# Attention weights of blocks 4 to 17 transposed by VectorE in 32x32 squares and moved by DMAs, not by TensorE

## The chip, the cores and the metric

The kernel runs on one core of one Trainium2 chip. A core has several engines, each with its own instruction queue: TensorE (PE, with PEld for its weight loads) multiplies matrices, VectorE (DVE) and ScalarE (ACT) work on 128 lanes of data, as GpSimd (POOL) does, and SyncE (SP) issues DMAs. Engines wait for one another by semaphores. TensorE writes its products to PSUM; SBUF is the memory from which all engines work. The metric is the device time of one execution in microseconds (us); lower is better.

## What is computed

Attention over chunks of 64 tokens (8 batches, 8 heads, 576 tokens of 64 values per head), whose result is the input of a feed-forward layer with a rational function between its two products:

```python
scores = scale * np.matmul(q_c, k_c.transpose(0, 1, 2, 4, 3))
scores = scores - np.max(scores, axis=-1, keepdims=True)
attn = np.exp(scores)
attn = attn / (np.sum(attn, axis=-1, keepdims=True) + 1e-09)
out = np.matmul(attn, v_c)
...
h = x @ w_in
h2 = h * h
h3 = h2 * h
P = a[0] + a[1] * h + a[2] * h2 + a[3] * h3
Q = 1.0 + np.abs(b[0]) * np.abs(h) + np.abs(b[1]) * h2
g = P / (Q + 1e-06)
return (g @ w_out).astype(np.float32)
```

Here `x` has 4608 tokens of 512 values, `w_in` is 512 x 2048 and `w_out` 2048 x 512.

## The kernel before

**Tiling.** The 4608 tokens go in 18 blocks of 256. For the attention a block is 32 score matrices of 64x64, kept as one tile of 128 partitions x 1024 columns. Its feed-forward part goes in four steps, s = 0 to 3, of 512 hidden columns each. Products of the feed-forward layer use numbers split in a high and a low part, three products for one (`xhi`, `xlo` with `wi_hi`, `wi_lo`; `ghi`, `glo` with `wo_hi`, `wo_lo`).

**The order of work.** Every engine takes its instructions in the order in which the program writes them, and that order is written by hand as strings of letters. `START` orders the first twelve steps; from step (3,0) on, step (n,s) runs the letters of `STEADY[s]` (L668). Letters of the attention that belong to the next block, m = n+1, are `n N T K A X Y`; `S M U E0 E1` belong to block n+2; `w o s h l` finish block n-1; the others are the feed-forward work of the step itself or, for `Z z y`, of two steps before. So the attention of one block is spread over some two blocks of feed-forward work:

- `S`: 32 products of 64x64 make the scores `pss`; `M` and `U` reduce them to maxima, `E0` and `E1` write the exponentials to the tile `e`.
- `n` (L278, L279): the reciprocals of the row sums; `N` (L284): DVE multiplies `e` by them.
- `T` (L309): TensorE transposes `e` in eight 128x128 pieces into the PSUM tile `pst`; `K` (L313): ACT copies it to the SBUF tile `at`.
- `A` (L214): 32 products of 64x64 of `v` with `at` make `psx`; the load of the next block's `v` is issued behind it. `X` and `Y` split `psx` into `xhi` and `xlo`, with which the first step of block m starts.

**The end of a block.** For blocks 5 to 16 the last quarter of the second product is done with seven products instead of eight (letter `V`, `ff2_seven`), and its result `o` is put together by `w`, one ACT copy (L532) and four DVE adds of 256 columns (L533 to L536), and by `o`, a DVE add of 1024 columns (L541). For earlier blocks `store` copies a whole `o` by ACT (L577). In both cases `put` (L583) then stores `o` with four DMAs on SP's queue, each of 64 partitions.

**Shared buffers.** `e`, `at` and `o` are tiles of one tag, `eo`, that has two slots, taken in turn in the order in which the program makes the tiles. A new tile waits until whatever read or wrote the old one in its slot is done. The PSUM tiles `pst` and `xacc` share the tag `pa`.

Letters `Q I J p P g H R G Gp` are the rational function: L373 to L407 on DVE and ACT, with `Gp` (L407) on POOL.

Of the kernel before, what the change touches and what calls it, by code (L numbers as in the profile page):

```python
# [10 lines left out]
F32 = mybir.dt.float32  # L11
# [8 lines left out]
P = 128  # L20
# [4 lines left out]
NQ = UPB * NHP  # L25
# [32 lines left out]
def tile_chunked_attention_rational_moe(  # L58
# [11 lines left out]
    nc = tc.nc  # L70
    cp = ctx.enter_context(tc.tile_pool(name="cp", bufs=1))
    p2 = ctx.enter_context(tc.tile_pool(name="p2", bufs=2))
# [19 lines left out]
    def bank_pair(tag, name):  # L92
        return ps.tile([P, 2, 512], F32, tag=tag, name=name)


    loaded = {}

    def load_qk(n, early=False):
        if n >= NB:
            return  # L100
        if n > 5:
            if n == 6:
                loaded["qk"] = p2.tile([P, 2, W], F32, tag="raw", name="qk", bufs=3)
            loaded["q", n], loaded["k", n] = loaded["qk"][:, 0, :], loaded["qk"][:, 1, :]
        elif early:
            q, k = (p2.tile([P, W], F32, tag=t, name=f"{t}qk{n}") for t in "AB")
        else:
            qk = p2.tile([P, 2, W], F32, tag="raw", name=f"qk{n}", bufs=3)
            q, k = qk[:, 0, :], qk[:, 1, :]
        if n < 6:  # L110
            loaded["q", n], loaded["k", n] = q, k
        if not early:
            load_part(n, slice(0, W))
# [5 lines left out]
    def load_v(n):  # L119
        if n >= NB:  # L120
            return
        v = p2.tile([P, W], F32, tag="vt", name=f"v{n}", bufs=1)
        nc.sync.dma_start(out=v, in_=vP[n])
        loaded["v", n] = v
# [77 lines left out]
    def groups_of(u):  # L202
        return slice(0, NQ) if u is None else slice(u * NHP, (u + 1) * NHP)

    before, cuts = [""], [(0, 0)]

    def quarters(out_cols, tile_out, stat, mov, u):
        before[0] = "quarters"
        for g in range(NQ)[groups_of(u)]:
            for par in range(2):  # L210
                for c in range(2):
                    rows = slice(64 * c, 64 * c + 64)
                    cols = slice(g * 128 + par * 64, g * 128 + par * 64 + 64)
                    nc.tensor.matmul(  # L214
                        tile_out[par * 64:(par + 1) * 64, c, out_cols(g)],
                        stat[rows, cols], mov[rows, cols], start=True, stop=True,
                    )

    att = {}


    def have(key, n, make):
        if (key, n) not in att:
            att[key, n] = make()
        return att[key, n]

    def spread(x):
        return x.unsqueeze(3).to_broadcast([P, 2, x.shape[2], 64])

    def att_s(n, u=None, tag="pa"):  # L230
        pss = have("s", n, lambda: bank_pair(tag, f"pss{n}"))
        quarters(lambda g: slice(g * 64, g * 64 + 64), pss, loaded["q", n], loaded["k", n], u)
# [4 lines left out]
    def stats(n, u):  # L237
        st = have("st", n, lambda: p2.tile([P, 3, 2, NQ], F32, tag="sm", name=f"sm{n}"))
        return (st[:, i, :, groups_of(u)] for i in range(3))

    def exps(n, u):
        e = have("e", n, lambda: p2.tile([P, NQ, 2, 64], F32, tag="eo", name=f"e{n}"))
        return e[:, groups_of(u), :, :]

    def by_group(e):
        return e.rearrange("p h c k -> p c h k")
# [31 lines left out]
        nc.vector.tensor_scalar(rs, sm, 1e-9, WS, ALU.add, ALU.mult)  # L278
        nc.vector.reciprocal(rs, rs)  # L279

    def att_norm(n, u=None):
        ec = by_group(exps(n, u))
        _, _, rs = stats(n, u)
        nc.vector.tensor_mul(ec, ec, spread(rs))  # L284

    def att_norm_act(n):
        e, (_, _, rs) = exps(n, None), stats(n, None)
# [14 lines left out]
    def part(u):  # L302
        return slice(0, W) if u is None else slice(u * W // 2, (u + 1) * W // 2)

    def att_t(n, u=None, tag="pa"):
        e = att["e", n]
        pst = have("t", n, lambda: bank_pair(tag, f"pst{n}")).rearrange("p a b -> p (a b)")
        for g in range(NQ)[groups_of(u)]:
            nc.tensor.transpose(pst[:, g * 128:(g + 1) * 128], e[:, g, :, :].rearrange("p c k -> p (c k)"), ident)  # L309

    def att_copy(n, u=None):
        at = have("at", n, lambda: p2.tile([P, W], F32, tag="eo", name=f"at{n}"))
        nc.scalar.copy(at[:, part(u)], att["t", n].rearrange("p a b -> p (a b)")[:, part(u)])  # L313
# [3 lines left out]
    def att_av(n, u=None, tag="pa"):  # L317
        psx = have("x", n, lambda: bank_pair(tag, f"psx{n}"))

        def cols(g):  # L320
            v, hp = divmod(g, NHP)
            return slice(hp * 128 + v * 64, hp * 128 + v * 64 + 64)

        quarters(cols, psx, loaded["v", n], att["at", n], u)


    def x_views(n, u):
# [89 lines left out]
    def seven(n, s):  # L417
        return s == NST - 1 and ST_FIRST <= n < NB - 1
# [4 lines left out]
    def t_tile(name, dtype=F32R):  # L423
        return p2.tile([P, 4, 2, 256], dtype, tag="raw", name=name, bufs=3)
# [3 lines left out]
    def t_home(k):  # L428
        if k == 0:
            tw["hi"], tw["lo"] = t_tile("thi"), t_tile("tlo")  # L430
        tw["sum"] = p2.tile([P, 2, 2, 256], F32, tag="eo", name=f"tsum{k}")
# [67 lines left out]
    def s_lo(n, engine=None):  # L499
        slo[n] = p2.tile([P, 4, 2, 128], F32R, tag="xlo", name=f"slo{n}")  # L500
        (engine or nc.vector).tensor_sub(slo[n], sums.pop(n), shi[n].bitcast(F32))
# [73 lines left out]
    def store(n):  # L575
        o = p2.tile([P, 2, DM], F32, tag="eo", name=f"o{n}")
        nc.scalar.copy(o, obuf.pop(n))  # L577
        put(n, o)
# [26 lines left out]
    def ph_tag(g):  # L605
        return "p1" if g == 1 or (g >= 10 and g % 2 == 0) else "p0"
# [45 lines left out]
    def run(program, then=""):  # L652
# [13 lines left out]
    total = len(steps)  # L666
    one = lambda names, k: run(" ".join(f"{x}{k}" for x in names.split()))
    STEADY = (  # L668
# [4 lines left out]
    )  # L673

    def step(g):
        n, s = steps[g]
        m = n + 1 if n + 1 < NB else None
        early = n + 2 if n + 2 < NB else None
        whole, fast = seven(n, NST - 1), seven(n - 1, NST - 1)
        of_m = {  # L680
            "n": att_rs, "N": att_norm, "Na": att_norm_act, "T": att_t, "K": att_copy, "X": att_xhi, "Y": att_xlo,
            "A": lambda k: (att_av(k, tag=ph_tag(g + 1)), load_v(k + 1)),
        }
        of_early = {"S": lambda k: (att_s(k), load_qk(k + 1)), "M": att_max, "U": att_sub,
                    "E0": lambda k: att_exp_half(k, 0), "E1": lambda k: att_exp_half(k, 1)}
        of_prev = {"s": s_sums, "h": s_hi, "l": s_lo, "lp": lambda k: s_lo(k, nc.gpsimd), "w": s_store, "o": s_out}
        other = {"Q": chain_nq, "I": chain_nln, "g": chain_t, "H": chain_inv, "R": chain_g, "G": chain_split, "Gp": chain_split}
        tokens = STEADY[s].split()
        for token in tokens:
            name = token.rstrip("'")  # L690
            late = token != name
            k = g - 1 if late else g
            if name == "B":
                if n in (3, 4):
                    t_make(n - 3)
                continue
            if name == "K" and n in (3, 4):
                t_home(n - 3)
            if name in of_m:
                if m is not None:  # L700
                    of_m[name](m)
            elif name in of_early:
                if early is not None:
                    of_early[name](early)
            elif name in of_prev:
                if fast:
                    of_prev[name](n - 1)
            elif name == "V":
                if fast:
                    ff2_seven(n - 1)  # L710
                    run(f"y{g - LAG - 1}", "F")
                else:
                    run(" ".join(f"{x}{g - LAG}" for x in "Zzy"), "F")
                    store(n - 1)
            elif name in "Zzy":
                if not (s == 0 and fast and name == "y"):
                    last = "z" if s == 0 and fast else "y"
                    run(f"{name}{g - LAG}", "F" if name == last else "z")
            elif late and s == 0 and fast and name in other:
                other[name](*steps[k])  # L720
            elif late and s == 0 and fast and name in ("L", "Lp"):
                chain_rest(*steps[k], nc.gpsimd if name == "Lp" else None)
            elif name in ("L", "Lp"):
                pass
            elif not late and s == 3 and whole and name in other:
                other[name](*steps[k])
            elif late and g == FIRST:
                pass
            elif name == "Gp" and (g == FIRST or n == NB - 1):
                run(f"G{g}")  # L730
            else:
                run(f"{name}{k}")
# [45 lines left out]
```

## Time and profile before

| | us |
|---|---|
| median of three runs | 869.49 |
| lowest and highest | 869.23, 869.64 |
| span of the profiled execution, first to last instruction | 866.8 |
| median less span | 2.7 |
| DVE busy (753 instructions) | 764.2 |
| ACT busy (972) | 575.5 |
| POOL busy (50) | 109.8 |

The times are of three runs without the profiler; the profile and the trace are of one execution with it, for which the span is what was recorded. In the trace a row of a timeline has the start from the span's begin, the duration, the engine, the line of the kernel, the operation, output and inputs, the shape and how many instructions the row covers, and in brackets how long the engine had been idle and what ended that. The durations of matmuls overlap, since they are pipelined. SPq and ACTq are the queues of DMA issues.

### The profile page before, as it was taken

How to read it: one execution, taken by the hardware profiler on the slowest of the kernel's cores; microseconds unless marked ns; L12 is line 12 of the kernel's file. 1: busy time of each engine (PE TensorE's matmuls, PEld its weight loads, DVE VectorE, ACT ScalarE, POOL GpSimd, SP SyncE). 2: the span in 40 equal slices, each digit the busy share in tenths (PEclk: the TensorE clock that was granted, in tenths of full speed). 3: DMA queues.
4: the chain of work that ended last, by engine and by line, in shares of the span. 5: the costliest groups of instructions: out<-in, count | busy, mean ns of one | idle time of the engine just before them, and what ended most of it. 6: DMA issues, size and time to landing. Idle time of an engine off the chain costs nothing.

```text
span 866.8 us, 21128 instructions
## 1 busy us (share of the span) xinstructions
PE 850.7 (98%) x9312; PEld 839.8 (97%) x9312; DVE 764.2 (88%) x753; ACT 575.5 (66%) x972; POOL 109.8 (13%) x50
## 2 busy tenths in 40 slices
PE   4999999999999999999999999999999999999997
PEld 3899999999999999999999999999999999999997
DVE  6999998897888898989989898989898989899985
ACT  5999865755848665858485757576666758584643
POOL 1222222001212111010111111111111110101100
PEclk9999999999999999999999999999999999999999
DMA  8753304012121202011121212121202020101010
GB/s 315 268 217 125 122 26 147 26 26 74 25 75 25 75 1 85 15 50 51 25 75 25 74 26 74 26 74 26 74 22 78 1 76 24 43 9 25 2 26 26
DMA packets 16509, 55.90 MB, mean 64 GB/s; under 512 B 2592, under 2 KB 2592, under 8 KB 14368
## 3 DMA queue, kind: packets, MB, share of 16 engines
q1 hardware_dynamic: 16256, 54.28, 19.2%
q8 instruction: 73, 1.20, 0.6%
q10 hardware_dynamic: 160, 0.26, 0.1%
q14 instruction: 20, 0.16, 0.1%
HBM read 45.09 MB, written 9.44 MB: 63 GB/s over the span
## 4 chain that ended last, share of the span: by engine, by line
PE 93%; DVE 4%; DMA 2%; issue 0%; SPq 0%; ACT 0%; DVEq 0%
PE ph L357 44%; PE po L566 36%; PE xacc L523 4%; PE po L523 3%; PE psx L214 2%; PE pss L214 2%; PE pst L309 2%; DMA raw<-in_w_in 1%; DMA v<-in_vP 1%; PE pl L193 1%; DVE ghi L394 0%; DVE B L402 0%; DVE C L389 0%; DVE B L373 0%; DVE B L398 0%
## 5 line engine op out<-in xcount | busy, mean ns | idle before, releaser
L357 PE MATMUL ph<-xhi,wi_hi 128*128 128x256 f32 x1152 | 321.4, 279 | 0.0
L357 PE MATMUL ph<-xlo,wi_hi 128*128 128x256 f32 x1152 | 318.9, 277 | 0.3 <-DVE xlo L340 0.3
L357 PE MATMUL ph<-xhi,wi_lo 128*128 128x256 f32 x1152 | 318.6, 277 | 0.0
L357 PEld LDWEIGHTS ph<-xlo,wi_hi 128*128 128x128 f32 x1152 | 216.7, 188 | 0.7 <-DVE xlo L340 0.6
L357 PEld LDWEIGHTS ph<-xhi,wi_hi 128*128 128x128 f32 x1152 | 216.3, 188 | 0.9 <-issue 0.8
L357 PEld LDWEIGHTS ph<-xhi,wi_lo 128*128 128x128 f32 x1152 | 216.5, 188 | 0.0
L566 PE MATMUL po<-wo_hi,ghi 128*128 128x256 f32 (+2 forms) x920 | 181.3, 278 | 0.0
L566 PE MATMUL po<-wo_lo,ghi 128*128 128x256 f32 (+2 forms) x920 | 179.7, 277 | 0.0
L407 POOL TENSOR_TENSOR glo<-B,A 128x1024 fp32r<-128x1024 f32 x36 | 91.0, 2529 | 659.9 <-DVE B L402 633.6
L566 PEld LDWEIGHTS po<-wo_hi,ghi 128*128 128x128 f32 x920 | 138.7, 188 | 0.9
L566 PEld LDWEIGHTS po<-wo_lo,ghi 128*128 128x128 f32 x920 | 138.8, 188 | 0.0
L377 ACT ACTIVATE A<-B,cst 128x1024 f32<-128x1024 f32 x60 | 69.3, 1154 | 91.2 <-DVE B L373 86.1
L361 ACT ACTIVATE A<-ph,ab 128x1024 f32<-128x1024 f32 x72 | 81.7, 1134 | 62.6 <-PE ph L357 59.0
L566 PE MATMUL po<-wo_hi,glo 128*128 128x256 f32 (+2 forms) x920 | 114.9, 277 | 0.0
L566 PEld LDWEIGHTS po<-wo_hi,glo 128*128 128x128 f32 x920 | 109.1, 188 | 0.2
L394 DVE SCALAR_TENSOR_TENSOR ghi<-C,ab,A 128x1024 fp32r<-128x1024 f32 x60 | 77.0, 1283 | 25.1 <-ACT A L381 20.4
L369 ACT ACTIVATE C<-ph,ab 128x1024 f32<-128x1024 f32 x72 | 88.6, 1231 | 10.1 <-PE ph L357 10.1
L389 DVE SCALAR_TENSOR_TENSOR C<-C,ab,ph 128x1024 f32<-128x1024 f32 x72 | 92.2, 1281 | 3.1 <-ACT B L365 0.7
L373 DVE SCALAR_TENSOR_TENSOR B<-B,ab,A 128x1024 f32<-128x1024 f32 x60 | 79.6, 1328 | 10.4 <-POOL glo L407 5.3
L385 DVE TENSOR_TENSOR C<-C,ph 128x1024 f32<-128x1024 f32 x72 | 87.4, 1214 | 0.5 <-ACT A L361 0.4
L381 ACT ACTIVATE A<-A,cst 128x1024 f32<-128x1024 f32 x72 | 83.1, 1154 | 2.2
L402 DVE SCALAR_TENSOR_TENSOR B<-C,ab,B 128x1024 f32<-128x1024 f32 x60 | 77.0, 1284 | 1.9
(138 smaller groups left out, 1148.1 us busy)
## 6 DMA issues: line engine op xcount, KB each, us to landing
v<-in_vP SPq DMA_DIRECT2D x18, 512.0 KB, 4.0
out<-o SPq DMA_DIRECT2D x68, 128.0 KB, 2.4
raw<-in_w_in SPq DMA_DIRECT2D x8, 1024.0 KB, 6.3
raw<-in_w_out SPq DMA_DIRECT2D x8, 1024.0 KB, 4.8
qk<-in_qT SPq DMA_DIRECT2D x16, 512.0 KB, 5.1
qk<-in_kT SPq DMA_DIRECT2D x16, 512.0 KB, 6.0
Aqk<-in_qT SPq DMA_DIRECT2D x2, 256.0 KB, 5.2
Bqk<-in_kT SPq DMA_DIRECT2D x2, 256.0 KB, 5.5
```

The costliest lines, as they stand in the source:

```text
L357: nc.tensor.matmul(ph[:, fi, :], w[:, cc, f], x[:, cc, :], start=(k == 0), stop=(k == len(mm) - 1))
L361: nc.scalar.activation(ch[n, s][1], ch[n, s][0], AF.Abs, scale=b0)
L369: nc.scalar.activation(ch[n, s][3], ch[n, s][0], AF.Identity, bias=a2, scale=a3)
L373: nc.vector.scalar_tensor_tensor(B, B, b1a, A, ALU.mult, ALU.add)
L377: nc.scalar.activation(A, B, AF.Ln, bias=cst[:, 0:1], scale=2.0 ** -KLN)
L381: nc.scalar.activation(A, A, AF.Exp, bias=cst[:, 1:2], scale=-1.0)
L385: nc.vector.tensor_mul(C, C, h)
L389: nc.vector.scalar_tensor_tensor(C, C, a1, h, ALU.add, ALU.mult)
L394: nc.vector.scalar_tensor_tensor(gbuf[n, s][0], C, a0, A, ALU.add, ALU.mult)
L402: nc.vector.scalar_tensor_tensor(B, C, a0, B, ALU.add, ALU.subtract)
L407: (engine or nc.vector).tensor_mul(gbuf[n, s][1], B, A)
L566: nc.tensor.matmul(accs[n][i][:, cols], g[:, fi, i * 128:(i + 1) * 128], w[:, FPS * s + fi, cols], start=start, stop=stop,)
```

## The change

From the steady part on, that is for blocks 4 to 17, the transposing is taken from TensorE. `T` is now `att_turn`: one DVE instruction transposes `e` in squares of 32x32, each in place among its neighbours, and writes them to a new tile `et`. `K` is now `att_move`: sixteen DMAs on SP's queue, each of 32 partitions by 256 columns, bring the squares from `et` to their places in `at`. `A` reads `at` in two runs of 32 columns for one of 64 (`split`). The normalisation is done by POOL (`Np`), ahead of `T`. `T` and `K` stand in the second step (s = 1) rather than in the third: `T` ahead of `w` and `o`, `K` behind `o`. `D` is the part of the old `K` that makes a buffer for `t_make` in steps n = 3 and 4. `et` is a further tile of tag `eo`.

```diff
--- before.py
+++ after.py
@@ -204,7 +204,7 @@
 
     before, cuts = [""], [(0, 0)]
 
-    def quarters(out_cols, tile_out, stat, mov, u):
+    def quarters(out_cols, tile_out, stat, mov, u, split=False):
         before[0] = "quarters"
         for g in range(NQ)[groups_of(u)]:
             for par in range(2):
@@ -213,7 +213,8 @@
                     cols = slice(g * 128 + par * 64, g * 128 + par * 64 + 64)
                     nc.tensor.matmul(
                         tile_out[par * 64:(par + 1) * 64, c, out_cols(g)],
-                        stat[rows, cols], mov[rows, cols], start=True, stop=True,
+                        stat[rows, cols], mov[rows, 2 * par:2 * par + 2, g, :] if split else mov[rows, cols],
+                        start=True, stop=True,
                     )
 
     att = {}
@@ -278,10 +279,10 @@
         nc.vector.tensor_scalar(rs, sm, 1e-9, WS, ALU.add, ALU.mult)
         nc.vector.reciprocal(rs, rs)
 
-    def att_norm(n, u=None):
+    def att_norm(n, u=None, engine=None):
         ec = by_group(exps(n, u))
         _, _, rs = stats(n, u)
-        nc.vector.tensor_mul(ec, ec, spread(rs))
+        (engine or nc.vector).tensor_mul(ec, ec, spread(rs))
 
     def att_norm_act(n):
         e, (_, _, rs) = exps(n, None), stats(n, None)
@@ -308,6 +309,22 @@
         for g in range(NQ)[groups_of(u)]:
             nc.tensor.transpose(pst[:, g * 128:(g + 1) * 128], e[:, g, :, :].rearrange("p c k -> p (c k)"), ident)
 
+    def att_turn(n):
+        e = att["e", n].rearrange("p g c k -> p (g c k)")
+        t = p2.tile([P, 4, NQ, 32], F32, tag="eo", name=f"et{n}")
+        nc.vector.transpose(t.rearrange("p j g r -> p g j r"), e.rearrange("p (g j k) -> p g j k", j=4, k=32))
+        att["et", n] = t
+
+    def att_move(n):
+        t = att["et", n]
+        att["at", n] = at = p2.tile([P, 4, NQ, 32], F32, tag="eo", name=f"at{n}")
+        for j in range(4):
+            for i in range(4):
+                nc.sync.dma_start(out=at[32 * j:32 * j + 32, i, :, :], in_=t[32 * i:32 * i + 32, j, :, :])
+        turned.add(n)
+
+    turned = set()
+
     def att_copy(n, u=None):
         at = have("at", n, lambda: p2.tile([P, W], F32, tag="eo", name=f"at{n}"))
         nc.scalar.copy(at[:, part(u)], att["t", n].rearrange("p a b -> p (a b)")[:, part(u)])
@@ -321,7 +338,7 @@
             v, hp = divmod(g, NHP)
             return slice(hp * 128 + v * 64, hp * 128 + v * 64 + 64)
 
-        quarters(cols, psx, loaded["v", n], att["at", n], u)
+        quarters(cols, psx, loaded["v", n], att["at", n], u, n in turned)
 
 
     def x_views(n, u):
@@ -666,9 +683,9 @@
     total = len(steps)
     one = lambda names, k: run(" ".join(f"{x}{k}" for x in names.split()))
     STEADY = (
-        "F f Gp' s a L' h b l Q c n N I p J P g H R Gp Z z y",
-        "F f a b c V w o Q I p J P g H R G",
-        "F f a b c Q Z z y T K I p J P g H R Gp",
+        "F f Gp' s a L' h b l Q c n Np I p J P g H R Gp Z z y",
+        "F f a b c T V w o K Q I p J P g H R G",
+        "F f a b c Q Z z y D I p J P g H R Gp",
         "F f A S a b X Y c M B Q U I p J P E0 E1 g H R Z z y",
     )
 
@@ -678,7 +695,7 @@
         early = n + 2 if n + 2 < NB else None
         whole, fast = seven(n, NST - 1), seven(n - 1, NST - 1)
         of_m = {
-            "n": att_rs, "N": att_norm, "Na": att_norm_act, "T": att_t, "K": att_copy, "X": att_xhi, "Y": att_xlo,
+            "n": att_rs, "N": att_norm, "Np": lambda k: att_norm(k, engine=nc.gpsimd), "T": att_turn, "K": att_move, "X": att_xhi, "Y": att_xlo,
             "A": lambda k: (att_av(k, tag=ph_tag(g + 1)), load_v(k + 1)),
         }
         of_early = {"S": lambda k: (att_s(k), load_qk(k + 1)), "M": att_max, "U": att_sub,
@@ -694,8 +711,10 @@
                 if n in (3, 4):
                     t_make(n - 3)
                 continue
-            if name == "K" and n in (3, 4):
-                t_home(n - 3)
+            if name == "D":
+                if n in (3, 4):
+                    t_home(n - 3)
+                continue
             if name in of_m:
                 if m is not None:
                     of_m[name](m)
```

On DVE, block 9's steps 0 and 1 (the transposed block is 10; the names are those of the tiles, with a running number at the end). Before:

```order
L278 TENSOR_SCALAR sm_5371<-sm_5371 128x16
L279 RECIPROCAL sm_5371<-sm_5371 128x16
L284 TENSOR_TENSOR e_5379<-e_5379,sm_5371 128x2x8x64
L385 TENSOR_TENSOR C_0_5513<-C_0_5513,ph_0_5447 128x1024
L389 SCALAR_TENSOR_TENSOR C_0_5513<-C_0_5513,ab,ph_0_5447 128x1024
L394 SCALAR_TENSOR_TENSOR ghi_0_5522<-C_0_5513,ab,A_0_5503 128x1024
L398 SCALAR_TENSOR_TENSOR B_0_5508<-B_0_5508,ghi_0_5522 128x1024
L402 SCALAR_TENSOR_TENSOR B_0_5508<-C_0_5513,ab,B_0_5508 128x1024
L533 TENSOR_TENSOR o_5674<-o_5674,xacc_5615 128x256
L534 TENSOR_TENSOR o_5674<-o_5674,xacc_5615 128x256
```

The same place on DVE in the changed kernel, where most of these lines stand 17 lines further down:

```order
L279 TENSOR_SCALAR sm_5419<-sm_5419 128x16
L280 RECIPROCAL sm_5419<-sm_5419 128x16
L402 TENSOR_TENSOR C_0_5561<-C_0_5561,ph_0_5495 128x1024
L406 SCALAR_TENSOR_TENSOR C_0_5561<-C_0_5561,ab,ph_0_5495 128x1024
L411 SCALAR_TENSOR_TENSOR ghi_0_5570<-C_0_5561,ab,A_0_5551 128x1024
L415 SCALAR_TENSOR_TENSOR B_0_5556<-B_0_5556,ghi_0_5570 128x1024
L419 SCALAR_TENSOR_TENSOR B_0_5556<-C_0_5561,ab,B_0_5556 128x1024
L315 STREAM_TRANSPOSE et_5663<-e_5427 128x8x4x32
L550 TENSOR_TENSOR o_5724<-o_5724,xacc_5665 128x256
L551 TENSOR_TENSOR o_5724<-o_5724,xacc_5665 128x256
```

The product with `sm` has left the place behind the reciprocal, and one transposing instruction has come between the last pass of step 0 and the adds on `o`.

On SP's queue, the stores of `o` of block 8, the copies for block 10, and the loads of `v`, `q` and `k` for later blocks. Before:

```order
L117 DMA qk<-in_kT 128x1024
L583 DMA out<-o_5674 64x512 x4
L123 DMA v_5904<-in_vP 128x1024
L117 DMA qk<-in_qT 128x1024
L117 DMA qk<-in_kT 128x1024
```

And in the changed kernel:

```order
L117 DMA qk<-in_kT 128x1024
L600 DMA out<-o_5724 64x512 x4
L323 DMA at_5735<-et_5663 32x256 x16
L123 DMA v_5960<-in_vP 128x1024
L117 DMA qk<-in_qT 128x1024
L117 DMA qk<-in_kT 128x1024
```

The sixteen copies stand between the four stores and the three loads. With `et` among the tiles of `eo`, `o` now takes the slot that `e` of the next block had, and `at` takes the slot of that `o`.

## The prediction

> **What bounds the kernel now.** I read the page first: busy time by engine, then the chain that ended last.
>
> ```profile
> span 866.8 us, 21128 instructions
> PE 850.7 (98%) x9312; PEld 839.8 (97%) x9312; DVE 764.2 (88%) x753; ACT 575.5 (66%) x972; POOL 109.8 (13%) x50
> PE 93%; DVE 4%; DMA 2%; issue 0%; SPq 0%; ACT 0%; DVEq 0%
> ```
>
> PE is busy for 98% of the span and carries 93% of the last chain. The next view cuts the middle of the run into stretches of one block each (from one `psx` product to the next); its columns are the stretch, its length, the busy time of PE, PEld, DVE, ACT and POOL with instruction counts, the granted clock, the DMA share and GB/s.
>
> ```profile
> 432.05:478.17 46.12, 46.12 (x516) 45.93 (x515) 41.40 (x43) 30.45 (x57) 4.81 (x2) 1.00 0.16 47
> ```
>
> A block costs 46.12 us and PE is busy for all of them, at a granted clock of 1.00. DVE has 4.7 us to spare, ACT 15.7. So time falls by what PE no longer does, as long as PE is not made to wait; and every wait of PE is paid in full.
>
> **What leaves PE.** The timeline of PE around block 10's transposes and around its `psx`:
>
> ```profile
> 471.74 1.04 PE L309 MATMUL pst<-ident,e 128*128 128x128 f32 x8
> 472.54 0.37 PE L357 MATMUL ph<-xhi,wi_hi 128*128 128x256 f32 x1
> 472.74 0.28 PE L357 MATMUL ph<-xlo,wi_hi 128*128 128x256 f32 x1
> ...
> 477.85 0.28 PE L357 MATMUL ph<-xlo,wi_hi 128*128 128x256 f32 x1
> 477.96 0.28 PE L357 MATMUL ph<-xhi,wi_lo 128*128 128x256 f32 x1
> 478.17 0.64 PE L214 MATMUL psx<-at,v 64*64 64x64 f32 x28
> ```
>
> The rows overlap since matmuls are pipelined, so I go by starts. From the first transpose to the second `ph` matmul are 472.74 − 471.74 = 1.00 us. Ordinary `ph` matmuls start 0.11 apart (477.85, 477.96). One such step would be there anyway, so the eight transposes cost 1.00 − 0.11 = 0.89 us. Fourteen blocks (4 to 17): 12.5 us. The profiled span is 866.8, and the median of the three runs, 869.49, stands 2.7 above it; I take those 2.7 to lie around the span and to stay. The floor of the change, with no new wait, is 869.5 − 12.5 = **857.0**.
>
> **What DVE, ACT and POOL exchange.** The timeline of DVE in step (9,1), with its ACT copy and the one POOL row there:
>
> ```profile
> 451.30 0.25 DVE L279 RECIPROCAL sm<-sm 128x16 f32<-128x16 f32 x1
> 451.58 1.23 DVE L284 TENSOR_TENSOR e<-e,sm 128x1024 f32<-128x1024 f32 x1
> 452.73 1.21 DVE L385 TENSOR_TENSOR C<-C,ph 128x1024 f32<-128x1024 f32 x1
> ...
> 457.97 1.28 DVE L402 SCALAR_TENSOR_TENSOR B<-C,ab,B 128x1024 f32<-128x1024 f32 x1
> 459.17 0.41 DVE L533 TENSOR_TENSOR o<-o,xacc 128x256 f32<-128x256 f32 x1
> ...
> 460.41 0.41 DVE L536 TENSOR_TENSOR o<-o,xacc 128x256 f32<-128x256 f32 x1
> 461.01 1.22 DVE L541 TENSOR_TENSOR o<-o,po 128x1024 f32<-128x1024 f32 x1 [0.19 <-PE po L566]
> ```
> ```profile
> 457.84 0.37 ACT L532 COPY o<-xacc 128x256 f32<-128x256 f32 x1 [0.27 <-PE xacc L523]
> ```
> ```profile
> 459.42 2.41 POOL L407 TENSOR_TENSOR glo<-B,A 128x1024 fp32r<-128x1024 f32 x1 [23.00 <-DVE B L402]
> ```
>
> The normalisation (L284, 1.23) goes to POOL. There a product of the same 128x1024 shape takes 2.41; it would run from about 451.6 to 454.1, and its reader comes at 458, so the chain from L385 to L402 hides it. The PSUM copy of `at` on ACT goes too; ACT has room, so it is worth nothing, nor is the bookkeeping letter `D`. [...]
>
> The turn in 32x32 squares is not in the trace. Near bounds are DVE's own passes over 1024 columns (1.21 to 1.28); the far ones are 0.69, which a plain one-input pass takes, and the 2.41 of POOL above.
>
> ```profile
> L162 DVE TENSOR_SCALAR raw<-raw 128x1024 int32<-128x1024 int32 x9 | 6.2, 691 | 1.8 <-DMA raw<-in_w_in 1.8
> ```
>
> I take 1.21: one column per lane and step, like the row that it replaces. DVE's load then stays as it was. Its place does not. The work up to L402 starts 1.15 us sooner (452.73 − 451.58), so L402 ends near 458.1 instead of 459.25, and the turn ends near 459.3. Only then is `e`'s slot free, into which `o` of the block before goes, so the ACT copy (0.37), which ran at 457.84, now follows the turn: the adds on `o` begin near 459.73 and end 1.65 later (459.17 to 460.82 before) at 461.4, and the last add starts there instead of at 461.01. **The finished `o` is 0.40 us later.**
>
> **What SP gets.** Here lies the cost. Sixteen copies of 32 partitions stand in SP's queue behind the four stores of `o`; `at` takes the slot of that `o`, so the first copy also waits until the last store has landed. And `psx`, the next product of PE, reads all sixteen. Rows of SP, the group's row of the page with its landing time last, and the load issues at the start of the run:
>
> ```profile
> 462.31 2.39 SPq L583 DMA_DIRECT2D out<-o  x4
> ```
> ```profile
> 462.31 0.47 SPq L583 DMA_DIRECT2D out<-o  x1
> ```
> ```profile
> 464.11 0.59 SPq L583 DMA_DIRECT2D out<-o  x1
> ```
> ```profile
> out<-o SPq DMA_DIRECT2D x68, 128.0 KB, 2.4
> ```
> ```profile
> 1.64 0.43 SPq L151 DMA_DIRECT2D raw<-in_w_in  x1
> 2.12 0.43 SPq L117 DMA_DIRECT2D Aqk<-in_qT  x1
> 2.59 0.43 SPq L117 DMA_DIRECT2D Bqk<-in_kT  x1
> ```
>
> A burst of four stores: the fourth starts 464.11 − 462.31 = 1.80 after the first and takes 0.59. The first issue takes 0.47 and the next follows at about 0.52, which leaves (1.80 − 0.52)/2 = 0.64 from one start to the next. Loads issued back to back stand at 2.59 − 2.12 = 0.47. What do SBUF-to-SBUF copies take? Like the stores they read SBUF and cover fewer than 128 partitions; so **I choose 0.64**, with 0.47 as the other end. The sixteenth copy then starts 0.52 + 14 x 0.64 = 9.48 after the first. For landing I estimate 2.0: the stores' 2.4 for 128 KB, less something for a quarter of the bytes. Bounds of it are 1.5 and 2.4, by the same row.
>
> The path from the last add's old end, 461.01 + 1.22 = 462.23, to `psx` at 478.17 was 15.94 us, all of it PE's own work; without the transposes it is 15.05. The new path beside it:
>
> - `o` later 0.40; from its end to the first store 0.08 (462.31 − 462.23)
> - to the start of the fourth store 1.80, its landing 2.4, release of SP 0.1 (estimate)
> - sixteen issues to the last start 9.48, landing 2.0
> - PE's eight extra semaphore waits ahead of `psx` 0.2 (estimate)
>
> The last term is half of 8 x 0.051, since waits already met run ahead of the matmuls; its ends are 0 and 0.4:
>
> ```profile
> L214 PEldq EVENT_SEMAPHORE  x2: 51/51/51, 476.1 to 478.9; - x2
> ```
>
> Sum 16.46 us, against 15.94 before: PE waits 1.41 us per block and loses 0.52 net. So the DMA path, and no longer PE alone, paces the block. This holds for blocks 7 to 17, where `o` goes through the adds: 11 x 0.52 = +5.7. Blocks 4 to 6 have the plain store of a whole `o` by ACT:
>
> ```profile
> 183.98 2.39 SPq L583 DMA_DIRECT2D out<-o  x4
> 201.31 0.33 SPq L123 DMA_DIRECT2D v<-in_vP  x1
> ```
> ```profile
> 200.09 0.29 PE L214 MATMUL psx<-at,v 64*64 64x64 f32 x4
> ```
>
> There 200.09 − 183.98 = 16.11 lay between the first store and `psx`; now 1.80 + 2.4 + 0.1 + 9.48 + 2.0 + 0.2 = 15.98. That is −0.13 each, −0.4 in all. Total 869.5 + 5.7 − 0.4 = **874.8 us**.
>
> What else is queued: behind the copies on SP stand the loads of `v`, `q` and `k`, but that of `v` waits for `psx` in any case (201.31 against 200.09), and a copy that waits holds up nothing else on SP. The `psx` product now reads `at` in two runs of 32 columns. The trace has no such read on PE; I take no cost, and at the far end a doubling of its some 0.7 us would add 10 us in all.
>
> [...]
>
> **The rivals.**
>
> *The copies keep ahead of PE (faster).* Place: SP's pitch. At 0.47 the sixteenth starts 0.52 + 14 x 0.47 = 7.1 after the first and the path is 14.1 < 15.05: no wait, 857.0. All of the path but the pitches is 16.46 − 14 x 0.64 = 7.50; 7.50 + 14p reaches 15.05 at p = 0.54, from which PE begins to wait, and 15.94 at p = 0.60, where gain and loss are equal. A landing of 1.5 shifts both points up by 0.04. For it: the loads' rows. Against: the 0.59 of three stores in four. Between 0.54 and 0.60 lie times from 857 to 869. This is the rival on the other side, and a close one: 0.04 us in the pitch turn the sign.
>
> *The turn is slow.* If DVE needs 2.41 rather than 1.21, `o` is ready 1.2 us later; at my pitch 11 x 1.2 = 13.2 come on top: 888. For it: the output is written in pieces of 32 columns with strides, which no row of DVE shows. Against: 1024 columns take DVE 1.21 to 1.28 in the rows above.
>
> *The issues are slower still.* If copies follow each other at 0.70, 14 x 0.06 = 0.84 us more per block, in 14 blocks 11.8: 887.
>
> **How the numbers follow.** Some 0.2% (1.7 us) is about what a measurement of this kernel can tell from no change; between 867.8 and 871.2 I call it the same. My forecast, DMA path behind PE at a pitch around 0.62 to 0.66, takes 0.40, and gives 871 to 878. The faster rival takes 0.33 (857 to 867.7), pitch or landing near break-even 0.14, the two slow rivals together 0.13. Range: 857 is a likely point and not a tail, so the low end lies just under it, at 856.5; the high end at 884 leaves out the slow rivals' full price, and a slow read on PE. Faster 0.33, same 0.14, slower 0.53.
>
> **What would show it.** The distance from one `psx` to the next is 46.12 now; I expect 46.6, and 45.2 if nothing waits. The first `psx` matmul should show about 1.4 us of idle PE, released by a DMA into `at`. SP should show sixteen starts at 0.64; under 0.54 I am wrong in sign. The last add should end 0.40 later against the block before, the turn should take 1.2, the landing 2.0. PE's matmuls should be 112 fewer. I would also be wrong if copies are not issued behind the landing of the stores, or if POOL's product ends after 458 and delays the turn.

## The result and the profile after

| | us |
|---|---|
| changed kernel, median of four runs (lowest, highest) | 879.70 (878.39, 880.69) |
| kernel before, median of four runs beside it | 869.57 |
| ratio of the times (95% interval) | 1.0111 (1.0095 to 1.0126) |
| span of the profiled execution, whose own time was 880.04 | 878.2 |

The change makes the kernel 1.1% slower, about 10 us. The span grew by 878.2 − 866.8 = 11.4 us. First the page of the changed kernel: span, busy time, and the chain that ended last, by engine and by line.

```profile
span 878.2 us, 21405 instructions
PE 850.5 (97%) x9200; PEld 836.9 (95%) x9200; DVE 766.2 (87%) x753; ACT 564.3 (64%) x958; POOL 134.2 (15%) x64
PE 62%; SPq 18%; DMA 9%; DVE 5%; ACT 3%; issue 3%; DVEq 0%; ACTq 0%
```

PE has 112 matmuls fewer, yet its busy time is nearly that of before. Without the copies (the first experiment) it is 839.7, so part of the wait is counted as busy here, and the chain says more: it was PE for 93% and is now PE for 62%, with 27% on SP's queue and on DMAs. The stretch from one `psx` to the next shows it for one block (columns as before: stretch, length, PE, PEld, DVE, ACT, POOL, clock, DMA share, GB/s):

```profile
435.02:481.89 46.87, 46.07 (x508) 45.62 (x507) 41.38 (x43) 29.64 (x56) 6.68 (x3) 1.00 0.19 58
```

46.87 us for 46.12 before, with eight matmuls less. The end of that stretch on SP, and then PE's `psx`:

```profile
466.87 2.43 SPq L600 DMA_DIRECT2D out<-o  x4
471.27 10.51 SPq L323 DMA_DIRECT2D at<-et  x16
484.25 0.33 SPq L123 DMA_DIRECT2D v<-in_vP  x1
```
```profile
481.68 0.28 PE L374 MATMUL ph<-xhi,wi_lo 128*128 128x256 f32 x1
481.89 0.47 PE L214 MATMUL psx<-at,v 64*64 64x64 f32 x6
483.11 1.05 PE L214 MATMUL psx<-at,v 64*64 64x64 f32 x57 [0.75 <-DMA at<-et]
```

The stores start at 466.87; the first copy is issued 4.40 later, and the sixteen issues take 10.51, to 481.78. PE begins `psx` at 481.89, gets six of 64 matmuls done, and can go on only at 483.11, when a DMA into `at` has landed. It is the same in all fourteen blocks: the last `psx` matmul starts 0.97 to 1.14 us after the last copy has landed, and an undisturbed `psx` takes 0.94 from its first start to its last. The groups of the issues and of the turn (name, count, shortest, median and longest duration in ns, first and last start; then the time from issue to landing of the copies):

```profile
L323 SPq DMA_DIRECT2D at<-et x224: 507/589/1988, 188.5 to 809.0; - x112
...
DMA to landing us min/median/max: 1.8/1.9/3.9
```
```profile
L315 DVE STREAM_TRANSPOSE et<-e x14: 1239/1239/1240, 181.0 to 788.1; 128x1024 f32<-128x1024 f32 x14
```

A copy's issue takes 0.589, as that of a store (0.588), and most follow each other at 0.63.

**Where the 11.4 us come from.** I read from the trace the distance between the last `psx` matmuls of neighbouring blocks, against the same distance before (46.80 for blocks 5 and 6, 46.12 for 7 to 17, 44.19 for block 4):

| part | change, us | forecast |
|---|---|---|
| blocks 4 to 6: 44.94, 47.97, 47.32 | +2.4 | −0.4 |
| blocks 7 to 16: mean 46.71 | +5.9 | +5.2 |
| block 17: 47.72 | +1.6 | +0.5 |
| from there to the end | +1.5 | 0 |

### The profile page after: what moved, and what is told of

Its sections match the earlier page's. It is cut to its first block, busy times and chain, and to the rows that moved or that the text cites. A ratio compares the mean times of both kernels' runs of the same rounds, so it can differ in the third digit from the quotient of the medians.

```text
span 878.2 us, 21405 instructions
## 1 busy us (share of the span) xinstructions
PE 850.5 (97%) x9200; PEld 836.9 (95%) x9200; DVE 766.2 (87%) x753; ACT 564.3 (64%) x958; POOL 134.2 (15%) x64
## 4 chain that ended last, share of the span: by engine, by line
PE 62%; SPq 18%; DMA 9%; DVE 5%; ACT 3%; issue 3%; DVEq 0%; ACTq 0%
PE ph L374 24%; PE po L583 24%; SPq L323 15%; PE xacc L540 4%; DMA out<-o 4%; DMA at<-et 3%; PE po L540 3%; SPq L600 3%; PE psx L214 2%; PE pss L214 2%; DVE o L558 2%; DMA raw<-in_w_in 1%; ACT e L298 1%; DMA v<-in_vP 1%; PE pe L583 1%
## 5 line engine op out<-in xcount | busy, mean ns | idle before, releaser
L424 POOL TENSOR_TENSOR glo<-B,A 128x1024 fp32r<-128x1024 f32 x36 | 88.7, 2465 | 437.7 <-DVE B L419 325.0
L390 DVE SCALAR_TENSOR_TENSOR B<-B,ab,A 128x1024 f32<-128x1024 f32 x60 | 82.2, 1371 | 10.4 <-POOL glo L424 5.3
```

What stands on the lines that cost most here:

```text
L390: nc.vector.scalar_tensor_tensor(B, B, b1a, A, ALU.mult, ALU.add)
L424: (engine or nc.vector).tensor_mul(gbuf[n, s][1], B, A)
```

## The experiments

The claim to test: the end of a block is paced by stores, landing, sixteen issues and landing, in a row on SP, and by nothing else of the change. The diffs are against the changed kernel, unless it is said otherwise.

**The copies left out.**

```diff
-        att["at", n] = at = p2.tile([P, 4, NQ, 32], F32, tag="eo", name=f"at{n}")
-        for j in range(4):
-            for i in range(4):
-                nc.sync.dma_start(out=at[32 * j:32 * j + 32, i, :, :], in_=t[32 * i:32 * i + 32, j, :, :])
+        att["at", n] = t
```

> The sixteen copies are left out and psx reads the turned tile where it lies, so the squares stay at their old places. Theory: all of the added time comes from the copies and what they wait for; the removal on TensorE is worth its full 0.89 us in 14 blocks: 857 (856 to 858). Rival (the turn on VectorE, the product on POOL or the read in two runs of 32 columns cost something themselves): 860 or more.

Measured: 857.62 us, ratio 0.9863 (0.9848 to 0.9878). Blocks 7 to 17 stand 45.27 apart, 0.85 less than before (0.89 forecast). So the turn on DVE, the product on POOL and the read in two runs of 32 columns cost nothing that shows in the time, and the removal on PE is worth what was worked out.

**The normalisation alone moved to POOL**, in the kernel before.

```diff
-            "n": att_rs, "N": att_norm, "Na": att_norm_act, "T": att_t, "K": att_copy, "X": att_xhi, "Y": att_xlo,
+            "n": att_rs, "N": lambda k: att_norm(k, engine=nc.gpsimd), "Na": att_norm_act, "T": att_t, "K": att_copy, "X": att_xhi, "Y": att_xlo,
```

> The kernel before, with only the normalisation moved to POOL. Theory: TensorE is never kept waiting, its transposes come 18 us after POOL is done: 869.5, no change within 0.2%. Rival (POOL's work takes SBUF access from VectorE and that shows): 872 or more.

Measured: 869.59 us, ratio 0.9998 (0.9988 to 1.0007), and the distances between blocks are those of before to 0.01 us. This part does nothing by itself.

**No stores ahead of the copies.**

```diff
     def put(n, o):
+        if 2 <= n <= 15:
+            return
```

> The stores of o for blocks 2 to 15, those that stand ahead of the copies, are left out, so these rows of the output are not written. Theory: the copies start when o is complete, 4.35 us sooner (1.83 to the start of the fourth store, 2.5 to its landing and the release), which is more than the 1.5 us per block that TensorE waits: 857 to 859. Rival (the stores are hidden beside the copies and only the sixteen issues count): 875 to 880.

Measured in one run: 857.99 us. The copies of block 10 start 29.66 after the last `psx` of block 9 (33.71 in the changed kernel), the last of them at 39.1, and PE does not wait. With the same sixteen issues, only begun sooner, the whole loss is gone; so it is the row of both that counts, not either alone. The copies begin when `o` is complete (its first store, in the run without copies, starts at 29.67), so `at` does take the slot of `o`; slots taken strictly in turn would have given it that of `et`.

**Twenty copies per block**, four of them issued twice.

```diff
-        for j in range(4):
+        for j in (0, 1, 2, 3, 3):
```

> Four of the copies are issued twice, twenty per block. Theory: each further copy costs its 0.63 us of issue in full, 4 x 0.63 x 14 = 35 us: 915 (912 to 922, the upper part if the granted clock drops more often). Rival (TensorE waits for a landing or for the turn rather than for issues): under 890.

Measured in one run: 940.54 us, more than the upper end. The issues do cost their time: the distance between blocks 7 to 16 rose from 46.7 to 51.0, of which 2.5 are four more issues. Most of the rest fits the granted clock, though no run keeps the two apart: the stores start some 1.6 later after the last `psx` (30.9 for 29.3), and 3.4 us at half the clock are 1.7 of PE's work.

```profile
core 0: 938.7 us, clock 0.972
```

The records show fourteen stretches at half the clock, one for each `psx`, that begin during it or within 0.3 us behind it; thirteen last 3.4 us and one 6.8. The granted clock after such a wait, in a window across one `psx`:

```profile
508.00:515.00 7.00, 3.71 (x108) 3.43 (x110) 1.41 (x2) 2.75 (x3) 2.34 (x1) 0.66 0.11 28
```

**Half of the copies on ScalarE's queue.**

```diff
+    def move_part(n, queue, half):
+        t, at = att["et", n], att["at", n]
+        for j in range(4):
+            for i in half:
+                queue.dma_start(out=at[32 * j:32 * j + 32, i, :, :], in_=t[32 * i:32 * i + 32, j, :, :])
...
-    "F f a b c T V w o K Q I p J P g H R G",
+    "F f a b c T V w o K Q I p J Kb P g H R G",
```

> Theory: sixteen issues at 0.63 us on one queue, behind the landing of four stores, set when psx can run. With eight of them on SP and eight on ScalarE's queue (issued behind the last exponential of that step) the eighth starts about 38 us after the last psx matmul of the block before, not 43.8, and lands at 40, ahead of the 45.2 at which TensorE would ask for it. So TensorE never waits and only the removed transposes count: 869.6 - 12.5 = 857, 857 to 859. Rival A (the later place of the adds on o, or POOL's product, is what costs): stays at 875 or more. Rival B (ScalarE pays for eight issues of 0.6 us, 5 us per block, and delays its own chain): 862 to 870.

Here `K` issues eight on SP and `Kb` eight on ACT. Measured: 887.1 us, ratio 1.0203 (1.0178 to 1.0228), slower than the change itself. The forecast missed: both its reading (no wait) and the size of rival B. The timelines of SP, ACT, DVE and PE around the wait of block 10:

```profile
477.49 5.71 SPq L328 DMA_DIRECT2D at<-et  x8
```
```profile
477.13 6.07 ACTq L328 DMA_DIRECT2D at<-et  x8
483.30 1.12 ACT L385 ACTIVATE A<-ph,ab 128x1024 f32<-128x1024 f32 x1 [6.93 <-DMA at<-et]
484.31 1.01 ACT L389 ACTIVATE B<-ph 128x1024 f32<-128x1024 f32 x1
```
```profile
485.43 1.28 DVE L397 SCALAR_TENSOR_TENSOR B<-B,ab,A 128x1024 f32<-128x1024 f32 x1 [3.83 <-ACT B L389]
486.63 1.21 DVE L409 TENSOR_TENSOR C<-C,ph 128x1024 f32<-128x1024 f32 x1
487.88 1.28 DVE L413 SCALAR_TENSOR_TENSOR C<-C,ab,ph 128x1024 f32<-128x1024 f32 x1
```
```profile
489.27 2.14 PE L214 MATMUL psx<-at,v 64*64 64x64 f32 x63 [2.02 <-issue]
```

Both queues are done issuing by 483.2, and by 484.8 all has landed. But ACT's next work, the first pass over `ph`, stands behind these 6.07 us of issuing; DVE waits for it (3.83), and so its last read of `ph` ends at 487.88 + 1.28 = 489.16. `psx` takes the PSUM buffer of that `ph` and starts at 489.27, right behind it. The row names no releaser for the 2.02 of waiting, but in all fourteen blocks `psx` starts 0.10 to 0.11 after this last read (L413) ends, and 2.5 to 4.5 after the last copy has landed. The wait has moved from the copies to ACT's chain; the sixteen copies themselves were no longer what PE waited for. In this run, too, the clock was at half for 3.4 us behind two of the waits, in blocks 5 and 10.

**The normalisation back on DVE.**

```diff
-"Np": lambda k: att_norm(k, engine=nc.gpsimd),
+"Np": att_norm,
```

> The normalisation is put back on VectorE, all else as in the changed kernel. Theory: the work up to the turn ends 1.15 us later, which uses up the 0.60 us that the last add on o waits for TensorE and leaves 0.58 in blocks 7 to 17 (+6.4 us) and 1.15 in blocks 4 to 6, where ScalarE's copy of o waits for the turn (+3.5): about 889. Rival (POOL's product slows VectorE by shared access, or the turn is not on the path): 879 to 881, no change.

Measured: 896.93 us, ratio 1.0309 (1.0292 to 1.0326); the rival falls, and the theory had the size too small. In block 10's stretch the turn starts 25.45 after the last `psx` instead of 24.03, so 1.42 later and not 1.15; the last add's wait takes up 0.49 of it, and the stores of block 8 start at 30.24 instead of 29.31. That is 0.93, not 0.58. There are also four stretches of 3.4 us at half the clock inside the run, which the theory did not have.

**Twelve copies**, the four squares that keep their partitions copied by POOL.

```diff
         for j in range(4):
+            rows = slice(32 * j, 32 * j + 32)
+            nc.gpsimd.tensor_copy(at[rows, j, :, :], t[rows, j, :, :])
             for i in range(4):
-                nc.sync.dma_start(out=at[32 * j:32 * j + 32, i, :, :], in_=t[32 * i:32 * i + 32, j, :, :])
+                if i != j:
+                    nc.sync.dma_start(out=at[rows, i, :, :], in_=t[32 * i:32 * i + 32, j, :, :])
```

> The four squares that stay on their own partitions are copied by GpSimd, and only the other twelve by DMAs on SP. Theory: the last of twelve starts 11 x 0.63 + 0.45 = 7.4 us after the first, 41.0 after the last psx matmul of the block before, and lands at 42.9, ahead of the 44.3 at which TensorE reaches psx: no wait, 857 to 859. Rival (TensorE's wait is not set by the number of issues, but by the late o, or by GpSimd's work): 870 or more.

Measured: 858.56 us, ratio 0.9861 (0.9838 to 0.9885): faster than both kernels. SP and POOL, the stretch of block 10, and its `psx`:

```profile
463.64 8.72 SPq L326 DMA_DIRECT2D at<-et  x12
```
```profile
463.68 4.82 POOL L323 COPY at<-et 32x256 f32<-32x256 f32 x4 [5.37 <-DMA out<-o]
```
```profile
428.83:474.10 45.27, 45.27 (x516) 45.08 (x515) 41.66 (x43) 29.55 (x57) 11.38 (x7) 1.00 0.19 57
```
```profile
473.93 1.16 PE L214 MATMUL psx<-at,v 64*64 64x64 f32 x64
```

All 64 matmuls run in one go. POOL's four copies lie beside SP's twelve issues.

**Twelve on SP, four on GpSimd's queue.**

```diff
-                nc.sync.dma_start(out=at[32 * j:32 * j + 32, i, :, :], in_=t[32 * i:32 * i + 32, j, :, :])
+                (nc.sync if j < 3 else nc.gpsimd).dma_start(out=at[32 * j:32 * j + 32, i, :, :], in_=t[32 * i:32 * i + 32, j, :, :])
```

> All sixteen squares go by DMAs, twelve issued by SP and four by GpSimd, which has little else to do. Theory: as with twelve copies, 857 to 860, since both queues end before TensorE reaches psx, if GpSimd takes less than 2 us for an issue. Rival (the DMA engines or the landings are the limit, not SP's issues): 875 to 880, as with sixteen on SP.

Measured: 859.87 us, ratio 0.9874 (0.9847 to 0.9901). The same sixteen DMAs are moved, so neither the DMA engines nor the landings set the wait in the changed kernel. POOL needs 0.51 for an issue:

```profile
466.23 2.01 POOL L323 DMA_DIRECT2D at<-et  x4 [5.78 <-DMA out<-o]
```

**Twelve copies, with the normalisation on DVE**, that is, both of these edits in one kernel: twelve copies, and `Np` as `att_norm`.

> Twelve copies, and the normalisation back on VectorE as in the run norm_on_dve. Theory: lateness costs only where the copies' path is the last to arrive. With twelve the last lands 1.4 us ahead of TensorE, so a turn that is 1.15 us later is still hidden: 858 to 861, where the same edit cost 17 us with sixteen. Rival (the normalisation on VectorE delays its other work, whose results TensorE needs): 866 or more.

Measured: 867.57 us, ratio 0.9973 (0.9964 to 0.9983). This missed. The rows of SP for the same block:

```profile
465.86 2.44 SPq L603 DMA_DIRECT2D out<-o  x4
470.25 8.26 SPq L326 DMA_DIRECT2D at<-et  x12
```

I had put the landing of the last copy 1.4 us ahead of PE, from a burst of 7.4. In the run with twelve copies the last issue starts 40.8 to 42.2 us after the last `psx` (blocks 8 to 12) and the last copy lands at 43.3 to 44.0, for a `psx` at 44.32: 0.3 to 1.0 us to spare. The edit makes the stores 0.8 to 1.5 later (30.4 to 31.2 for 29.65), the last issue starts at 42.8 to 43.7, the last copy lands at 44.6 to 45.6, and `psx` is held up by 0.3 to 1.3 in these blocks. So the mechanism stands and the margin was taken too large. The rival, that the product delays other work of DVE, sets the end of `psx` in none of blocks 5 to 17: in all of them the last `psx` matmul starts 0.98 to 1.03 after the last copy has landed, as in the changed kernel, where the copies hold PE up. In blocks 5 to 7 PE also waits ahead of the first `psx` matmul, by up to 1.13, for something that the rows do not name.

## Why the prediction was right, and where it was off

The sign, the place and the mechanism came out as forecast, and 879.7 lies in the range; the loss is 10.1 us by the medians where 5.3 was forecast. By its own steps:

- **PE's saving**: 0.89 us per block forecast, 0.85 in the run without copies; the floor of 857.0 was reached at 857.6.
- **The pitch of the copies**: 0.64 chosen, 0.63 measured for most of them; the nearest row was that of the stores (0.588 us for an issue), not that of the loads (0.43 at the start of the run): a copy's issue takes 0.589.
- **The landing**: 2.0 against 1.9. **The turn**: 1.21 against 1.24. **Release after the stores**: 2.5 against 2.5 (31.14 to 33.65).
- **`o` later by 0.40**: right without a wait of PE, wrong with it. In the run without copies the first store starts 29.67 after the last `psx`, 0.35 later than before. In the changed kernel it starts at 29.31, as before, since DVE goes on while PE waits in `psx` and so comes to the turn 0.8 earlier by PE's count. This took 0.4 off the forecast.
- **The sixteen issues, 9.48**: they take 10.14 in the mean of blocks 7 to 16. This term was too small: in each burst one issue, the ninth to the eleventh, takes 1.05 or more instead of 0.59. It cost 0.66 per burst.
- **PE's eight extra waits, 0.2**: the last `psx` matmul starts 1.03 after the last landing in the mean of blocks 7 to 17, for 0.2 + 0.94 = 1.14 forecast, so this term was nearer 0.1.
- **The net loss of 0.52 in blocks 7 to 16**: 0.59 measured, but partly by luck, since errors cancel: 0.52 − 0.40 for `o`, + 0.66 for the burst, − 0.1 for the landing and − 0.1 for the waits are 0.58. By the prediction's own 0.52 + 14p a burst of 10.14 is a pitch of 0.69, next to the rival of still slower issues (0.70, 887 us). That the time did not come out near it is owed to `o`, which was no later.
- **Blocks 4 to 6, −0.4**: the step that failed. It took the store of a whole `o` to stand where it stood. But that `o` takes the slot of `e` as well, so ACT's copy waits for the turn:

```profile
231.44 1.02 ACT L594 COPY o<-po 128x1024 f32<-128x1024 f32 x1 [2.63 <-DVE et L315]
```

The first store of these blocks came 0.39, 1.08 and 0.35 later, and with the longer burst the three cost +2.4 instead of −0.4.

- **Nothing after the last block**: also off. The `psx` of block 17 waited longest (its burst took 11.1 from the first start to the last), and then PE ran at half its clock. The rows of PE, and of the 3.4 us behind them:

```profile
808.61 0.32 PE L214 MATMUL psx<-at,v 64*64 64x64 f32 x2
809.69 0.53 PE L214 MATMUL psx<-at,v 64*64 64x64 f32 x4 [0.76 <-DMA at<-et]
810.92 1.11 PE L214 MATMUL psx<-at,v 64*64 64x64 f32 x58 [0.70 <-DMA at<-et]
```
```profile
811.90:815.30 3.40, 3.40 (x22) 3.34 (x16) 2.19 (x2) 2.12 (x2) 0.67 (x1) 0.50 0.00 0
```

Half the clock for 3.4 us is 1.7 us of PE's work, about the +1.5 of the table. This part is not in every execution: two of the other three timed ones had a mean clock of 0.999 and 1.000, too high for such a stretch (3.4 us at half of 878 take off 0.002), and took 878.39 and 879.36.

Of the rivals, the one in which the copies keep ahead of PE gives the right time for its condition: with twelve issues it is the case, and the time is 858.6. The point of decision, 0.54 in pitch for sixteen, was passed by 0.09. That a slow turn or a slow read on PE is to blame is excluded by the run without copies.

## What to carry over

The chain of many small DMAs on one queue was priced here by its issues, sixteen in 10.14 us: count them, multiply by the pitch of the nearest kind of DMA in the trace (here the stores' 0.63 us, not the loads' 0.47), and add what the first of them waits for through a shared buffer. Compare that with the time until the engine at the bound asks for the result; taking four of sixteen issues away turned a loss of 10 us into a gain of 12. Here a second queue helped only on an engine that had little due behind the issues: on ScalarE 6.07 us of issuing eight copies cost more than they saved (887.1 us), on GpSimd the 2.01 us of issuing four cost little (859.87).

## What was not expected of the hardware

**An issue that lasts longer beside an instruction load.** In all fourteen bursts of the changed kernel one issue took 1.05 to 1.99 us, and each time a 16 KB DMA of the queue named "instruction", 0.93 to 1.53 us long, ran at that moment. One such issue, and the DMA queues in the same 1.2 us:

```profile
476.93 1.05 SPq L323 DMA_DIRECT2D at<-et  x1
```
```profile
q1 hardware_dynamic: 91, 0.06, 20.9%
q8 instruction: 1, 0.02, 4.8%
```

All the long issues of the runs with twelve copies (12), with twenty (14) and without stores (6) fall on such a load too. In these three runs 38 loads overlap a burst; the six that leave no long issue begin less than 0.25 us before the burst's end. In the changed kernel four such loads come in each block, 8 to 15 us apart, and one of them falls in each burst. Whether it is the load that holds up the issue was not tried.

**The granted clock after a short wait.** In block 17, with 2.3 us of waiting in and around `psx` (3.20 from its first matmul to its last, 0.94 before), the clock was 0.50 for the next 3.4 us (811.9 to 815.3); after waits of 1.1 to 2.0 in the other blocks it stayed at 1.00. With about 4 us per block (twenty copies, 3.8 to 5.0) it fell in every block. The length of the wait alone does not decide it: with the normalisation back on DVE it fell with 2.5 us in block 7 (`psx` runs from 347.02 to 350.42, and the stretch at half the clock begins at 349.65) and stayed at 1.00 after 2.9 in block 10 (490.89 to 494.71). What decides it, no run shows.
